# Transposing the normed rows on TensorE instead of by DMA, with row 32 of W loaded later and new instruction orders

## The chip, the core and the metric

The kernel runs on one core of a Trainium2 chip. A core has TensorE (called PE in the profile; its weight loads are PEld), VectorE (DVE), ScalarE (ACT), GpSimd (POOL) and SyncE (SP), each with its own in-order stream of instructions, the memories SBUF and PSUM (eight banks of 128 x 512 float32), and 16 DMA engines that serve the transfers that the engines issue. The metric is the time of one execution on the device in microseconds; the kernel before takes 343.75 us, the median of three runs (343.66 to 343.83).

## What is computed

The input x has 2048 rows of 512 values in bf16. Two layers are applied, each a spectral part A and a mixing MLP B, and each part adds to its own input:

```python
def A(x, w_r, w_i):                       # after a layer norm
    X = rfft2(x)                          # over rows and columns
    return irfft2(X * (w_r + 1j * w_i))   # W is 2048 x 257
def B(x, w1, w2, w3, w4):                 # after a layer norm
    h = gelu(layernorm(x) @ w1)           # 512 x 512
    hs = shifted(h) @ w2                  # four column groups, rows shifted by 1, -1, 2, -2
    x1 = x + hs
    return x1 + gelu(layernorm(x1) @ w3) @ w4   # 512 x 1792, 1792 x 512
for _ in range(2):
    x = x + A(layernorm(x), w_r, w_i)
    x = x + B(layernorm(x), w1, w2, w3, w4)
```

## The kernel before

The 2048 rows lie in SBUF as 16 groups of 128 (`K.x[:, q, :]`, called row q below; row 16p + q of x is on partition p). Everything stays in SBUF; x, W, tables and weights come in once by DMA, and only the last x goes out.

The rows' Fourier transform, the columns' transform, the product with W, and the inverse transforms are all matmuls with tables. In the first front, `scaled_T` multiplies the table T with each row's inverse standard deviation (operation Q in the orders), `front` (O) multiplies it with two rows at once on TensorE, and `take_front` (G, L, I) brings the result from PSUM to V, split between ACT and DVE. The transform proper follows: d and q (matmuls at lines 588 to 612), t and x (their evictions), p (the product with W), b (line 642), m and l (evictions into hT), D and C (line 662), Y (eviction), P (line 690) and a (adds to x, line 698).

The MLP begins with the norm of each row: s sums the squares on ACT (line 303), r works out the scale on POOL, n normalizes a row into the tile xn on ACT, DVE or POOL. The product with w1 needs the normed rows with their columns on partitions. Therefore `tr` (T) transposes two rows, one DMA for eight 128 x 128 blocks, into a tile xT that holds four rows:

```python
def turn(to, k, rows):
    ...
    nc.sync.dma_start_transpose(to[g][:, 2 * h:2 * h + 2].rearrange("p q t c -> p (q t) c"),
                                rows.rearrange("p q d -> p (q d)"))
```

v multiplies w1 with xT (line 733, 512 columns), h is the gelu into hT, u multiplies with w2 (line 749), f adds (line 757). The second norm (k, R, o) is followed by a second transpose, `tr3` (U, eight per layer, also line 718), and then by w (line 784), g (gelu into gT, line 791), W (line 804) and A (adds to x, line 810). E adds the middle of the MLP to x. In layer 1, S, Q, O, G and so on then begin the next layer's front, interleaved with the last w and W; in layer 2, y stores the rows.

No scheduler orders this. `ORDER_0` (first front), `ORDER_A` (layer 1) and `ORDER_B` (layer 2) list the operations, and each engine executes its share in the order of that list, waiting on semaphores. In an entry such as `n5A` the number is the row or unit, and a last letter A, V, P or D says which engine does it (ACT, DVE, POOL, or DVE directly from PSUM); in `w3.6` the 6 is the first PSUM bank. `X5.0` issues five filler matmuls on zeros; thirty more run at the start (`WAKE`). The letters in `FLEX` are those that carry an engine.

SP's queue issues the eight loads of x, then sixteen of W, then, after the small transfer gate2 that waits for the last doubling of W (lines 185 and 210), the tables G and Tinv and the weights w1, w2, w3, then the transposes in their order, w4 behind the eighth transpose of layer 1 (`load_w4`), and the stores. ACT's queue issues the table T and the two loads of row 32 of W (line 175) at the start. POOL's queue issues the tables FL, TL and TR at the entry f2 of ORDER_0 (`load_tables`) and the doubling copies of W after the first front (`load_rest`).

Of the kernel before, what the change touches and what calls it, by code (L numbers as in the profile page):

```python
# [28 lines left out]
def dft_tables():  # L29
# [39 lines left out]
    for j in range(NH):  # L69
        for sg in range(2):  # L70
# [26 lines left out]
           "Tinv": np.stack([T.T, -T.T], axis=1)}  # L97
# [59 lines left out]
def load_all(K, A_x, A_w_r, A_w_i, B_w1, B_w2, B_w3, B_w4):  # L157
    nc = K.nc
# [15 lines left out]
    for pl, v in enumerate(planes):  # L174
        nc.scalar.dma_start(K.W[2::4, pl, 0], v[:, 32])
    for lo in range(0, NH, 8):
        for pl, v in enumerate(planes):
            load_W(K, v, pl, lo, lo + 8)
    K.TL = K.const.tile([P, 2, NB, P], BF16, name="TL")
# [28 lines left out]
    def load_mlp():  # L208
        gate2 = K.const.tile([1, 16], BF16, name="gate2")
        nc.sync.dma_start(gate2[:], K.W[1:2, 1, NH - 1, 1:17])  # L210
        for k in ("G", "Tinv"):
            table(k, nc.sync)
        for k, w, n, c in (("w1", B_w1, 4, D), ("w2", B_w2, 4, D), ("w3", B_w3, 4, FH), ("w4", B_w4, 14, D)):
            t = K.const.tile([P, n, c], BF16, name=k)
            setattr(K, k, t)
            if k != "w4":
                load_halves(t, w, n)

    def load_w4():
        load_halves(K.w4, B_w4, 14)  # L220
# [5 lines left out]

    K.load_w4 = load_w4
# [260 lines left out]
def first_front(K):  # L488
# [66 lines left out]
    dummy = K.const.tile([P, 1, P], BF16, name="dummy")  # L555
    K.nc.sync.dma_start_transpose(dummy[:], K.zeros[:])
# [11 lines left out]
def layer(K, last):  # L568
# [144 lines left out]
    def turn(to, k, rows):  # L713

        g, h = divmod(k, 2)
        if g not in to:
            to[g] = K.grp.tile([P, 4, 4, P], BF16, name="xT", bufs=4)
        nc.sync.dma_start_transpose(to[g][:, 2 * h:2 * h + 2].rearrange("p q t c -> p (q t) c"),
                                    rows.rearrange("p q d -> p (q d)"))

    def tr(k):
        turn(xT, k, xn[:, 2 * k:2 * k + 2, :])
        turned.append(k)
        if len(turned) == 8 and not last:
            K.load_w4()
# [48 lines left out]
    def tr3(k):  # L774
        q = ROWS[2 * k]
        turn(xT3, k, xn[:, q:q + 2, :])
# [84 lines left out]
    def act_table(k):  # L861
# [42 lines left out]
FLEX = "mlGLnotxYIKEpQ"  # L904
FOLD = [(), ()]
ORDER_0 = """
s1 f0 s0 s3 s2 i3 i2 i0 s4 s5 S1 J1 s7 S0 J0 s6 i7 f2 Q2A Q3A i4 Q0A s9 i6 s8 O1.2 s11 f3 S2 J2 Q6P Q1A Q5A O0.4 i8
G1A Q4V O2.0 s10 i11 i10 S3 Q7P O3.2 G0A s13 J3 Q10V Q11A s12 s14 i12 O5.6 i14 G3A i13 G2A Q8P Q9P s15 S4 J4 O4.4 G5A
i15 Q12V Q13V S5 O6.0 L5A J5 Q14P O7.6 G4A G6A G3V Q15V L6V G7A O8.0 L7A G8A I3V L8A
"""  # L910
ORDER_A = """
d0.3 t0A d2.4 d1.2 d4.0 q0.6 t1V N0 t2A q1.2 d6.4 t4A q2.0 x1V x0V p1V t6A q4.2 d12.6 d10.4 x2A p2P p0V t12A t10A d8.0
p4D b0.6 d14.7 q10.4 m0V q6.2 t8A x10A t14A b1.0 b5.1 m5A m1A q12.4 q14.6 p6D b4.1 b2.0 p10V x14A p14P d15.2 m4A m2A
t15A q8.6 x8A b3.1 b7.0 m7A b11.2 q15.6 m11A x15A b10.3 b14.0 m3A b6.2 m6A p12D V12.4 b12.5 p8V p15V b13.7 b9.1 m10A
m12A b8.6 b15.2 m13V V15.3 m14V m9A m8V V13.5 V14.0 m15A D1.6 l12V D0.1 l15A l13A l14V C1 C0 Y0V Y1A D3.3 C3 P3.0 a3
P2.6 Y3A a2 s3 P0.5 a0 s2 P1.2 a1 s0 D2.0 C2 Y2V s1 r0 D5.6 C5 P7.2 a7 Y5A e0 s7 P6.4 D7.0 P4.5 a6 i0 M0 P5.2 D4.6 C4
P10.3 s6 C7 n2P a4 s4 a5 n3V n0V s5 Y4A D6.4 r1 P11.2 C6 P8.6 P9.7 e1 n1V a10 T1 Y7A P15.0 i1 M1 n5A s10 n4P n6P P14.1
Y6V P13.3 a8 s8 T0 a9 n7P s9 a11 P12.4 a15 s11 v1.6 r2 n10P T2 h1 T3 a13 a12 n11V c0 s15 T5 n8V v0.2 h0 s13 v3.4 n9V
v2.2 h3 u0.0 s12 h2 u1.4 a14 c1 s14 T4 u3.1 r3 f0 k0 n14V v5.2 n13A n15V T7 f1 E1V h5 f3 v4.6 u2.0 f2 E2V h4 c2 u6.6
f6 u5.5 f5 E5V k3 E6V n12P u7.0 E0V u4.1 f4 T6 v7.5 k2 k1 R0 E3V o2V o1V h7 o3A c3 v6.1 h6 o0P f7 u8.0 f8 E8P u13.5  # L920
u12.2 u11.6 u14.3 U1 f12 k4 k5 k7 f14 E14V k12 k6 u9.2 f11 u10.4 k8 E7V f13 k13 f10 R1 o7P o5P u15.3 E10V U0 w4.0 E4P
f9 E9P k11 f15 w2.4 g2 k10 o4V U2 w1.2 k14 g4 E15P k9 E13P w3.6 g3 g1 w5.0 w0.4 g0 w6.6 g5 g6 E11V W1.2 o6P U3 E12V A1
W3.6 A3 B3 B1 w8.0 W2.4 A2 W0.2 k15 R2 o10P o11A R3 o14V o9A g8 o12A w13.0 U5 w7.6 B2 g13 o8P U4 w15.4 w10.0 A0 B0 g10
w16.2 j1 g7 g16 w18.0 g18 w9.2 o15P w11.0 g9 w12.2 g12 j3 w17.6 j2 j0 S0 Q3V Q1V Q2P Q0V g11 W4.2 U7 O1.0 o13P g17 U6
A4 W7.3 B4 j4 G1A G1V A7 B7 j7 O0.0 w19.6 G0A W6.2 A6 g19 W5.3 A5 g15 B5 w23.4 g23 j5 B6 j6 S1 Q4P G0V w27.2 g27 I0V
w14.6 g14 Q5V O2.0 w20.2 w24.6 g20 W10.2 A10 B10 Q7V j10 W8.3 G2A A8 B8 W9.4 A9 B9 Q6V j9 W11.2 A11 w26.4 I1P B11 j11
g24 j8 O3.2 w22.6 S2 Q10P g26 G2V I2P Q11A Q8P g22 w21.0 g21 G3A w25.6 G3V g25 W12.0 A12 B12 j12 Q9P S12 J12 I3P O4.5
G4A Q12A G4V W15.1 A15 I4P B15 j15 W13.2 A13 S15 J15 B13 j13 W14.3 Q15P W24.2 S13 J13 Q13P O5.0 A14 A24 B14 B24 j14
G5A O15.4 G15V O6.2 S14 J14 L15A Q14A O14.4 G6A L6A G14A G5V I5V L14A
"""  # L930
ORDER_B = """
X6.7 d4.4 d15.7 t15A d12.2 t4V d1.0 d0.1 q15.4 t1V q4.6 t12A x15V q1.2 t0A x4A d2.0 p15P p1D q0.4 p0D q12.6 d10.2 t2A
x12A d8.0 q2.4 d6.6 t10A b1.3 p4V b5.2 t8A t6A q8.0 m1A m5A q6.6 p12P p2D x6A q10.3 b0.2 x10A b3.5 b2.6 m2A b4.7 m4A
d14.4 t14A p8D b9.1 m9A b13.0 p6V b12.3 p10V b7.6 m13A m7A m0A b6.4 q14.0 b15.7 b10.6 m3V b8.2 b11.5 m15A p14D b14.7
m12A m8V m14V V12.0 V14.1 V15.3 V13.2 m10A m6A l14V m11A l12A D2.5 l15V l13A D3.0 C3 Y3A C2 D1.2 C1 Y2V Y1A P7.1 a7
P6.0 a6 P4.5 P5.7 P2.2 P3.3 D0.0 s7 a4 s6 C0 a5 D5.4 s4 s5 r1 C5 a3 s3 Y0V D6.6 a2 e1 P0.0 P1.2 i1 a0 a1 Y5A P10.1 M1
n4V n5P D4.4 C4 P11.0 s2 T2 s0 n7V n6V T3 s1 r0 a10 a11 Y4A C6 e0 i0 D7.2 C7 P9.1 Y6A M0 n0P P8.4 Y7A P12.0 s11 n1V T0
a8 s10 P13.5 a9 s9 n3V n2P T1 c0 P15.2 a15 s8 P14.3 a14 s15 r2 n11V v3.1 h3 v2.3 h2 v0.6 h0 n10P T5 v1.2 a13 s13 n8P
h1 u0.4 s14 n9V T4 u3.5 a12 c1 u1.0 s12 r3 f3 u2.7 f1 k1 n14V n15P T7 f0 v5.2 c3 f2 v4.0 n13A h5 u4.3 n12V T6 f4 E3V
k0 h4 E1V u6.7 c2 u7.6 f7 k3 E0V u5.1 k2 R0 E7V E2V o1P o2P f5 E5V k4 v6.5 h6 o0A v7.0 h7 u13.6 o3V U1 u12.4 u15.5 f6  # L940
E6P f13 E13P u14.3 f14 k7 k5 E14V k6 R1 o7A E4V u11.0 f15 f12 k14 k12 u9.2 E15P f9 k13 o6V u8.1 u10.3 f10 E10V f11
E11V k15 U0 w6.4 w4.2 g4 k9 f8 E8V R3 o15A E12V o13V k10 w5.0 w1.2 g5 o12P k11 g1 w2.6 w0.1 g2 o14V g0 k8 R2 o11V o8P
w3.6 U3 g3 o5A U6 U7 w26.0 w21.2 g21 w22.6 g26 w23.2 E9V o9P g6 W0.0 A0 o4V U2 W3.1 W2.0 g23 g22 w25.2 W1.4 g25 w11.2
# [34 lines left out]
```

## Time and profile before

| | |
|---|---|
| median of three runs | 343.75 us (343.66 to 343.83) |
| profiled execution | 343.63 us, its span 341.8 us |
| TensorE busy | 334.3 us, 2184 matmuls |
| ACT, DVE, POOL busy | 192.0, 163.5, 117.5 us |
| granted TensorE clock | 1.00 throughout |
| DMA transposes | 32, 3.1 us each from issue to landing |

The profile shows one execution. Busy time of TensorE rests on modelled ends of matmuls, so the rate is read from how many matmuls pass in a stretch. "Idle before" in the groups is how long the engine stood still before these instructions, with what released it. The chain of waits is followed back from the last instruction, and a row of it gives start, length, engine, line and count. The groups by form keep different shapes of one line apart. The windows give each engine's busy time in a stretch of the span.

### The profile page before, as it was taken

How to read it: one execution, taken by the hardware profiler on the slowest of the kernel's cores; microseconds unless marked ns; L12 is line 12 of the kernel's file. 1: busy time of each engine (PE TensorE's matmuls, PEld its weight loads, DVE VectorE, ACT ScalarE, POOL GpSimd, SP SyncE). 2: the span in 40 equal slices, each digit the busy share in tenths (PEclk: the TensorE clock that was granted, in tenths of full speed). 3: DMA queues.
4: the chain of work that ended last, by engine and by line, in shares of the span. 5: the costliest groups of instructions: out<-in, count | busy, mean ns of one | idle time of the engine just before them, and what ended most of it. 6: DMA issues, size and time to landing. Idle time of an engine off the chain costs nothing.

```text
span 341.8 us, 5734 instructions
## 1 busy us (share of the span) xinstructions
PE 334.3 (98%) x2184; PEld 186.8 (55%) x2184; DVE 163.5 (48%) x373; ACT 192.0 (56%) x356; POOL 117.5 (34%) x218
## 2 busy tenths in 40 slices
PE   6999999999999999999999999999999999999996
PEld 4878984444444444444467898444444444444443
DVE  4979895659034023535378979456901110200112
ACT  6989899665821542421628979986695132142310
POOL 3795067669633000402432505877722000000000
PEclk9999999999999999999999999999999999999999
DMA  7985936390231100000000003543130500000011
GB/s 261 313 284 197 339 78 117 71 270 19 46 61 31 32 0 0 2 0 0 2 0 2 2 3 64 104 83 61 33 61 0 125 31 0 15 17 32 15 63 46
DMA packets 45340, 24.60 MB, mean 72 GB/s; under 512 B 35153, under 2 KB 42321, under 8 KB 45313
## 3 DMA queue, kind: packets, MB, share of 16 engines
q1 hardware_dynamic: 43824, 19.74, 23.0%
q0 software_dynamic: 1248, 4.40, 3.9%
q8 instruction: 17, 0.28, 0.3%
q10 hardware_dynamic: 240, 0.10, 0.1%
q14 instruction: 11, 0.08, 0.1%
HBM read 11.61 MB, written 2.10 MB: 40 GB/s over the span
## 4 chain that ended last, share of the span: by engine, by line
PE 85%; ACT 8%; DVE 3%; DMA 2%; issue 1%; SPq 0%; ACTq 0%
PE ps L804 28%; PE ps L784 28%; PE ps L749 8%; PE ps L733 6%; PE ps L642 4%; ACT xn L303 3%; PE ps L612 2%; PE ps L594 2%; DVE x_state L698 2%; PE ps L662 2%; DMA x_state<-in_A_x_dram 1%; ACT hT L740 1%; DMA xT<-xn 1%; PE ps L439 1%; PE ps L429 1%
## 5 line engine op out<-in xcount | busy, mean ns | idle before, releaser
L791 ACT ACTIVATE gT<-ps 128x1024 bf16<-128x1024 f32 x56 | 55.7, 1023 | 97.6 <-PE ps L784 95.5
L804 PE MATMUL ps<-w,gT 128*128 128x512 bf16 (+2 forms) x476 | 99.4, 366 | 0.0
L784 PE MATMUL ps<-xT,w 128*128 128x512 bf16 x448 | 99.3, 379 | 0.0
L810 DVE TENSOR_TENSOR x_state<-ps,x_state 128x512 bf16<-128x512 f32 (+2 forms) x34 | 22.1, 659 | 123.4 <-PE ps L804 123.1
L804 PEld LDWEIGHTS <-gT 128*128 128x128 bf16 x476 | 45.4, 98 | 51.4
L784 PEld LDWEIGHTS <-w 128*128 128x128 bf16 x448 | 43.7, 98 | 52.1
L757 DVE SCALAR_TENSOR_TENSOR xn<-xn,ln_c,ps 128x512 bf16<-128x512 bf16 x32 | 23.3, 742 | 16.0 <-PE ps L749 6.3
L733 PE MATMUL ps<-xT,w 128*128 128x512 bf16 x128 | 28.6, 379 | 0.4 <-DMA xT<-xn 0.4
L749 PE MATMUL ps<-w,hT 128*128 128x512 bf16 x128 | 28.8, 379 | 0.1
L326 POOL TENSOR_SCALAR ln_ve<-ln_mv 128x4 f32<-128x4 f32 x11 | 3.0, 271 | 57.7 <-DVE ln_mv L319 57.0
L303 ACT ACTIVATE junk<-xn 128x512 bf16<-128x512 bf16 x32 | 19.8, 623 | 5.0 <-DVE xn L757 5.0
L291 DVE BATCH_NORM_STATS2 ln_st<-x_state 128x6 f32<-128x512 bf16 (+2 forms) x30 | 19.5, 665 | 3.5 <-DMA x_state<-in_A_x_dram 3.0
L698 DVE SCALAR_TENSOR_TENSOR x_state<-ps,x_state 128x512 bf16<-128x512 f32 x32 | 20.6, 684 | 0.9 <-PE ps L690 0.9
L733 PEld LDWEIGHTS <-w 128*128 128x128 bf16 x128 | 12.4, 98 | 15.6 <-DMA xT<-xn 1.0
L749 PEld LDWEIGHTS <-hT 128*128 128x128 bf16 x128 | 12.5, 98 | 15.4 <-ACT hT L740 1.0
L303 ACT ACTIVATE xn<-x_state 128x512 bf16<-128x512 bf16 x32 | 19.9, 626 | 0.8 <-DVE x_state L698 0.8
L740 ACT ACTIVATE hT<-ps 128x512 bf16<-128x512 f32 x32 | 17.6, 600 | 4.6 <-PE ps L733 4.5
L690 PE MATMUL ps<-Y,Tinv 128*128 128x256 bf16 x128 | 15.8, 272 | 0.4 <-DVE Y L152 0.4
L631 POOL TENSOR_TENSOR PB<-X,W 128x2048 bf16<-128x2048 bf16 (+1 forms) x4 | 12.1, 3033 | 11.2 <-DVE X L152 7.3
L154 ACT ACTIVATE TV<-ps 128x1024 bf16<-128x1024 f32 (+1 forms) x17 | 14.6, 895 | 2.4 <-PE ps L594 2.3
L642 PE MATMUL ps<-TR,PB 128*128 128x128 bf16 x256 | 15.9, 219 | 0.0
L662 PE MATMUL ps<-G,hT 128*128 128x256 bf16 x128 | 15.6, 273 | 0.0
(96 smaller groups left out, 414.0 us busy)
## 6 DMA issues: line engine op xcount, KB each, us to landing
w<-in_B_w_dram SPq DMA_DIRECT2D x4, 896.0 KB, 7.0
W<-W POOLq DMA_DIRECT2D x4, 514.0 KB, 5.1
x_state<-in_A_x_dram SPq DMA_DIRECT2D x8, 256.0 KB, 4.9
out_dram<-x_state SPq DMA_DIRECT2D x15, 128.0 KB, 1.8
w<-in_B_w_dram SPq DMA_DIRECT2D x4, 256.0 KB, 4.4
W<-in_A_w_r_dram SPq DMA_DIRECT2D x7, 128.5 KB, 5.4
W<-in_A_w_i_dram SPq DMA_DIRECT2D x7, 128.5 KB, 5.6
TL<-tab_TL POOLq DMA_DIRECT2D x3, 256.0 KB, 5.5
```

Of the source, the lines that this page charges most:

```text
L303: K.nc.scalar.activation(out, src, ACT.Square, bias=0.0, scale=D ** -0.5, accum_out=self.s[:, i, 1:2])
L642: nc.tensor.matmul(o[:, k0 * P:(k0 + 1) * P], lhsT=pab[u][:, k, 2 * (b - u) + h, f * P:(f + 1) * P], rhs=K.TR[:, k:k + 2, 2 * b + h], star ...
L662: nc.tensor.matmul(o[:, i, e * 256:(e + 1) * 256], lhsT=M[:, F, e, 2 * m + i, :], rhs=K.G[:, F, e, :], start=(F == 0 and e == 0), stop=(F ...
L698: nc.vector.scalar_tensor_tensor(K.x[:, q, :], ps.pop(("P", q)), 1.0, K.x[:, q, :], op0=ALU.mult, op1=ALU.add, accum_out=ln[g].s[:, i, 0:1])
L733: nc.tensor.matmul(o[:, i], lhsT=K.w1[:, t, j * P:(j + 1) * P], rhs=xT[g][:, :, t, :], start=(t == 0), stop=(t == 3))
L740: nc.scalar.activation(hv[:, 2 * h + i, 4 * g:4 * g + 4, PAD:PAD + P], o[:, i].rearrange("p (q c) -> p q c", q=4), ACT.Gelu_apprx_tanh, bi ...
L749: nc.tensor.matmul(o, lhsT=K.hT[:, j, st:st + P], rhs=K.w2[:, j, :], start=(j == 0), stop=(j == 3))
L757: nc.vector.scalar_tensor_tensor(xn[:, q, :], xn[:, q, :], ln[q // 4].c[:, q % 4:q % 4 + 1], ps.pop(("u", n)), op0=ALU.mult, op1=ALU.add, ...
L784: nc.tensor.matmul(o[:, i], lhsT=K.w3[:, c, t * P:(t + 1) * P], rhs=xT3[g][:, :, c, :], start=(c == 0), stop=(c == 3))
L791: nc.scalar.activation(gT[g][:, 2 * j:2 * j + 2, :], ps.pop(("w", k)), ACT.Gelu_apprx_tanh, bias=0.0, scale=1.0)
L804: nc.tensor.matmul(o, lhsT=gT[g][:, t, i * P:(i + 1) * P], rhs=K.w4[:, t, d], start=(t == 0), stop=(t == 13))
L810: nc.vector.tensor_tensor(x, ps.pop(("W", n)), x, op=ALU.add)
```

## The change

The turn is done by matmuls: eight for a pair of rows, each with a 128 x 128 block of rows as the stationary operand and the unit matrix as the moving one, into two PSUM banks. One copy of 128 x 1024 then brings it from PSUM to xT, on ACT or DVE; it is a new entry of the order, Z for the first and F for the second norm. The unit matrix is one more table, loaded on SP behind Tinv. The transposing DMA `dummy`, issued once ahead of the others, is gone, and w4 is loaded straight behind w3. Row 32 of W is loaded on SP behind the first four loads of W. All three orders are new: beside the Z and F entries they change the sequence throughout, and deal some operations to other engines (in layer 1, for instance, nine norms n go to POOL instead of six and five to DVE instead of eight). Layer 1 gets five fillers at its beginning, and layer 2 loses six.

```diff
-           "Tinv": np.stack([T.T, -T.T], axis=1)}
+           "Tinv": np.stack([T.T, -T.T], axis=1), "unit": np.eye(P)}
...
-    for pl, v in enumerate(planes):
-        nc.scalar.dma_start(K.W[2::4, pl, 0], v[:, 32])
     for lo in range(0, NH, 8):
         for pl, v in enumerate(planes):
             load_W(K, v, pl, lo, lo + 8)
+        if lo == 0:
+            for pl, v in enumerate(planes):
+                nc.sync.dma_start(K.W[2::4, pl, 0], v[:, 32])
...
-        for k in ("G", "Tinv"):
+        for k in ("G", "Tinv", "unit"):
             table(k, nc.sync)
         for k, w, n, c in (("w1", B_w1, 4, D), ("w2", B_w2, 4, D), ("w3", B_w3, 4, FH), ("w4", B_w4, 14, D)):
             t = K.const.tile([P, n, c], BF16, name=k)
             setattr(K, k, t)
-            if k != "w4":
-                load_halves(t, w, n)
-
-    def load_w4():
-        load_halves(K.w4, B_w4, 14)
+            load_halves(t, w, n)
...
-    dummy = K.const.tile([P, 1, P], BF16, name="dummy")
-    K.nc.sync.dma_start_transpose(dummy[:], K.zeros[:])
...
-    def turn(to, k, rows):
-
-        g, h = divmod(k, 2)
+    def turn(key, rows):
+
+        ps[key] = o = banks(K, 2)
+        for i in range(2):
+            for t in range(4):
+                nc.tensor.matmul(o[:, i, t * P:(t + 1) * P], lhsT=rows[:, i, t * P:(t + 1) * P], rhs=K.unit[:],
+                                 start=True, stop=True)
+
+    def take_turned(to, key, eng):
+        g, h = divmod(key[1], 2)
         if g not in to:
             to[g] = K.grp.tile([P, 4, 4, P], BF16, name="xT", bufs=4)
-        nc.sync.dma_start_transpose(to[g][:, 2 * h:2 * h + 2].rearrange("p q t c -> p (q t) c"),
-                                    rows.rearrange("p q d -> p (q d)"))
+        copy(K, to[g][:, 2 * h:2 * h + 2].rearrange("p q t c -> p q (t c)"), ps.pop(key), eng)
 
     def tr(k):
-        turn(xT, k, xn[:, 2 * k:2 * k + 2, :])
-        turned.append(k)
-        if len(turned) == 8 and not last:
-            K.load_w4()
+        turn(("T", k), xn[:, 2 * k:2 * k + 2, :])
...
     def tr3(k):
         q = ROWS[2 * k]
-        turn(xT3, k, xn[:, q:q + 2, :])
+        turn(("U", k), xn[:, q:q + 2, :])
...
-             "T": tr, "v": w1, "h": gelu1, "u": w2, "f": add_x1, "k": square3, "E": resid,
+             "T": tr, "Z": lambda k, eng: take_turned(xT, ("T", k), eng), "F": lambda k, eng: take_turned(xT3, ("U", k), eng), "v": w1, "h": gelu1, "u": w2, "f": add_x1, "k": square3, "E": resid,
...
-FLEX = "mlGLnotxYIKEpQ"
+FLEX = "mlGLnotxYIKEpQZF"
 ORDER_0 = """
-s1 f0 s0 s3 s2 i3 i2 i0 s4 s5 S1 J1 s7 S0 J0 s6 i7 f2 Q2A Q3A i4 Q0A s9 i6 s8 O1.2 s11 f3 S2 J2 Q6P Q1A Q5A O0.4 i8
...
+s1 f0 s0 i0 s2 i2 s3 i3 s8 s5 S0 J0 S1 J1 s9 s10 i8 s11 Q2A Q3A O1.6 i10 Q1A s12 i11 Q0P s15 f3 S3 J3 Q10A i12 s13 s4
+Q11A i13 s7 i4 Q8A O0.1 G0A s6 i6 S4 G1A J4 Q12V i7 Q9P O5.3 f2 L5A s14 S2 J2 Q4V Q7V i15 Q13A O4.0 Q6P O6.6 i14 Q5P
...
 ORDER_A = """
-d0.3 t0A d2.4 d1.2 d4.0 q0.6 t1V N0 t2A q1.2 d6.4 t4A q2.0 x1V x0V p1V t6A q4.2 d12.6 d10.4 x2A p2P p0V t12A t10A d8.0
...
-P10.3 s6 C7 n2P a4 s4 a5 n3V n0V s5 Y4A D6.4 r1 P11.2 C6 P8.6 P9.7 e1 n1V a10 T1 Y7A P15.0 i1 M1 n5A s10 n4P n6P P14.1
-Y6V P13.3 a8 s8 T0 a9 n7P s9 a11 P12.4 a15 s11 v1.6 r2 n10P T2 h1 T3 a13 a12 n11V c0 s15 T5 n8V v0.2 h0 s13 v3.4 n9V
...
+X5.0 d1.0 d0.1 t0A d2.2 t2A d10.6 t10A N0 t1V q0.4 q1.0 p0D q2.2 d6.6 d14.4 x2A d15.5 q10.2 p1D t6A q6.0 t14A q14.6
...
+a6 P4.7 a4 Y5V Y4A D6.0 n0V C6 s6 n1P P14.5 P8.4 P15.6 P9.7 s4 T0.2 Y6A P12.1 P13.0 a15 r1 e1 i1 n3A a9 a8 n2P T1.6
+a14 M1 n6P Z0A Z1A P10.2 a10 P11.3 a11 s8 s9 n7P s10 s11 n5V T3.4 Z3V a12 v1.6 h1 n4P r2 n8P n9P c1 T2.2 Z2V v0.4 v3.2
...
 ORDER_B = """
-X6.7 d4.4 d15.7 t15A d12.2 t4V d1.0 d0.1 q15.4 t1V q4.6 t12A x15V q1.2 t0A x4A d2.0 p15P p1D q0.4 p0D q12.6 d10.2 t2A
...
+d0.2 d1.0 t1V d15.4 d12.6 q1.0 t0A d4.2 p1D t15A t12A t4A q0.4 d2.6 q15.0 t2A p0D q4.2 q12.4 d6.6 x15V p4D d8.0 x12A
...
```

## The prediction

> **What bounds the kernel now.** I read the busy row of the page first, then the chain of waits, then the groups by form, then windows of time, because the busy row alone can't be trusted for TensorE: ends of matmuls are modelled in it.
>
> ```profile
> PE 334.3 (98%) x2184; PEld 186.8 (55%) x2184; DVE 163.5 (48%) x373; ACT 192.0 (56%) x356; POOL 117.5 (34%) x218
> PE 85%; ACT 8%; DVE 3%; DMA 2%; issue 1%; SPq 0%; ACTq 0%
> ```
>
> TensorE is named by both. How full it really is I work out from its true rate, which the chain of waits shows in runs of equal matmuls:
>
> ```profile
> 97.37 1.73 PE ps L784 x8
> 178.35 0.45 PE ps L439 x8
> 199.53 2.62 PE ps L662 x24
> ```
>
> The first row gives 216 ns for a 512-column matmul, the third 109 ns for 256 columns, the second 56 ns for 128 columns, where every matmul has its own weight load. (The "mean ns" column says 379, 273 and 219 for the same three: that is latency, not rate.) The groups by form count 1124 matmuls of 512 columns (L784, L804, L749, L733), 28 of 384 (4.9/28, at most 0.17 each), 392 of 256, 476 of 128, 128 half-height ones at L612 (16 in 0.98 us of the chain, 0.061 each) and 36 fillers of 256. So the streams need 242.8 + 4.6 + 42.7 + 26.7 + 7.8 + 3.9 = 328.5 us. The first matmul starts at 1.0 us and the last ends at 339.1: of 338.1 us only about 10 are not streaming. The start holds 4 of them: 30 fillers worth 3.3 us stand in the 7.2 us before the first real matmul at 8.23. **Some 6 us are left in the other 330.**
>
> ```profile
> 8.23 2.14 PE L429 MATMUL ps<-Tq,x_state 128*128 128x256 bf16 x24 [1.90 <-ACT Tq L412]
> ```
>
> Where those 6 lie, windows of time tell (columns: window, length, then busy us and count of PE, PEld, DVE, ACT, POOL, then the granted clock, the DMA share, GB/s):
>
> ```profile
> 8.20:19.00 10.80, 10.04 (x121) 9.03 (x120) 10.28 (x35) 10.76 (x25) 8.86 (x15) 1.00 1.01 321
> 19.00:36.00 17.00, 16.88 (x244) 13.92 (x245) 14.74 (x19) 15.89 (x26) 10.94 (x10) 1.00 0.70 229
> 36.00:62.00 26.00, 25.74 (x193) 17.86 (x191) 18.12 (x49) 23.15 (x55) 13.58 (x34) 1.00 0.59 160
> 62.00:180.00 118.00, 118.00 (x607) 56.22 (x606) 52.96 (x125) 51.46 (x85) 40.05 (x69) 1.00 0.17 38
> 200.00:216.00 16.00, 15.26 (x131) 12.53 (x130) 13.05 (x37) 14.14 (x34) 6.68 (x18) 1.00 0.31 56
> ```
>
> From 62 us to 180 us (and again after 216) TensorE never pauses and the others idle half the time. Only in the first front (to 19 us), the transforms and the first half of the MLP are ACT and DVE nearly full beside it. The clock is 1.00 throughout.
>
> **What the DMA transposes cost now.** Their rows:
>
> ```profile
> xT<-xn SPq DMA_TRANSPOSE x32, 3.1
> L733 PE MATMUL ps<-xT,w 128*128 128x512 bf16 x128 | 28.6, 379 | 0.4 <-DMA xT<-xn 0.4
> 211.02 3.50 DMA xT<-xn
> ```
>
> 32 transposes, 3.1 us each from issue to landing, and TensorE idles for them 0.4 us in all; one stands on the chain, at the start of layer 2's MLP. Their work is on the DMA engines and SP, which are free. So the removal gives back 0.4 us, with what surrounds that one wait at most 0.7 (16.00 less 15.26 in the last window shown above).
>
> **Added: turns on TensorE.** Each of 8 turns of xn and 8 of the second norm, in 2 layers, makes 8 matmuls, a stationary 128x128 block each, against the unit matrix: 32 x 8 = 256 matmuls of 128 columns. The nearest row is L439: 8 matmuls, the stationary operand a 128x128 block of bf16 rows, 128 columns moving, 0.45 us. 32 x 0.45 = **14.4 us**, on the engine that has no room: half of it falls in w3 and W work where no pause exists, half beside norms where pauses come to about 1 us a layer. Here a rule has to be weighed. The Trainium skill ("TensorE: Matmul & The Clock Gate", Part 4: PE-mode transpose) measures 390 ns for such a transpose in isolation and about 275 ns within a kernel, and says the clock gate doesn't count that mode as work. By 275 ns, 256 turns are an estimated 70 us, and the kernel ends near 414. I take the row: it is the rate of back-to-back ordinary matmuls, and the diff uses ordinary ones; 275 resembles the row's latency of 219 ns, which pipelining hides. A second page looks only at the pair of engines: "VectorE: DVE Perf Modes" (Rules for kernel authors, with its three transpose paths) prefers TensorE, 390 against 1309 ns for DMA. By that 256 x 919 ns = 235 us would be an estimated saving; the wait row allows 0.4. A price off the path can't be saved.
>
> **Added: copies.** 32 evictions of 128x1024 f32. Rows of the same shape:
>
> ```profile
> L154 ACT ACTIVATE Y<-ps 128x1024 bf16<-128x1024 f32 x11 | 11.1, 1015 | 2.6 <-PE ps L662 1.4 <-issue 1.1
> L152 DVE CAST Y<-ps 128x1024 bf16<-128x1024 f32 x5 | 6.1, 1223 | 3.1 <-PE ps L662 3.0
> ```
>
> The new orders put 16 on ACT (16.2 us), 16 on DVE (19.6). The second norm's 16 stand beside w3, where both engines idle half the time: nothing. The first norm's in layer 1 are 4 on ACT (4.06 us) and 4 on DVE, in a stretch where the chain runs from 40.85 to 59.43 through ACT and TensorE has no pause either. TensorE grows by 8 x 0.45 = 3.6 there, ACT by 4.1: the difference, **0.4**; between 0 (three normings more go to POOL) and 2 (a copy waits for its turn behind a gelu of two 0.6 us pieces, with v queued behind it on TensorE). In layer 2 only 2 of 8 are on ACT, so TensorE stays the longer one. A turn plus its copy, 0.45 + 1.0 to 1.2, is shorter than 3.1 us plus the 1.25 us of an SP issue, so the wait at 211 should shrink: **-0.5**, between -0.7 and +1 (an unready norm now holds TensorE itself, where before it held SP's queue only: u and v stand behind the turn).
>
> **New order of the first front.** ACT is full in that window (10.76 of 10.80), so its order sets when V is whole. Before, ACT makes the first two row scalings (Q2, Q3) before row 9's sums:
>
> ```profile
> 7.67 1.30 ACT L412 ACTIVATE Tq<-T,ln_r 128x256 bf16<-128x256 bf16 x3
> 8.88 0.61 ACT L366 ACTIVATE junk<-x_state 128x512 bf16<-128x512 bf16 x1
> 15.72 3.41 ACT L154 ACTIVATE V<-ps 128x512 bf16<-128x512 f32 x7
> ```
>
> Now s9 stands ahead of Q2, and s8 on DVE ahead of J0. Rows 8 and 9 are in the fifth load of x: issued near 2.6 us, landed after 4.9 to 5.3, so 7.5 to 7.9. ACT then sums for 1.3 us and begins Q2 near 9.2 instead of 7.67. The sums aren't lost (they'd have come at 8.88), so the loss is ACT's idleness: 0.3 us waiting for rows 8 and 9, and about 1 us before S3, whose group now waits on DVE for s8, J0, J1, s10, s11 and two aggregations. One scaling more (0.46) and one take fewer (0.6 to 0.9) cancel. +1.3, less what earlier x gives: row 32's two issues leave ACT's queue, 33 KB, 0.1 us at 321 GB/s, up to 0.5 if such small packets hold the queues longer than their bytes. I take **+0.9**, between -0.5 and +2.0. The five fillers ahead of layer 1 lie in that wait; six fewer at layer 2: **-0.1** by count (36 to 35 at 109 ns), up to -0.7.
>
> **Moved issues.** Row 32's two loads take 0.62 us each on SP, ahead of 12 W loads: these issue 1.25 us later. What they feed waits on POOL's doubling copies, the first at 17.1 us; row 32 should land by about 13.5, with 3.5 us cover; if it were gone, the transforms would start that much later. POOL's tables (FL, TL, TR) are issued at f2, which now stands behind f3, Q0, Q9: near 12.7 instead of 7.95. At the old 5.7 us FL lands near 18.4, at 2 to 3 us less without queueing; the transform wants it near 20. TL's second half follows 2.4 us of POOL work and could be late for q10, which the new order takes fourth: **+0.3**, between -0.5 and +1.5, for the whole transform stretch with its re-dealt takes. W4's load goes from behind the eighth transpose to behind w3, 0.9 MB twice, long before W at 91 us; the unit matrix (32 KB, one SP issue of 0.43) delays w1 by as much, and v starts at 51 us, over ten later than w1's landing: both nothing.
>
> **Sum.** 14.4 + 0.4 - 0.5 + 0.9 - 0.1 + 0.3 = 15.4 us. The profiled execution took 343.63 with a span of 341.8; it becomes 359.0 with a span of 357.2. The median of the runs is 343.75, 0.1 above it: **359.1 us**.
>
> **Rivals.** (1) The new orders also take back pauses: half of the 6 us that remain outside the start. For it: ACT in the chain at 40 to 59, the pauses in 200 to 216. Against: after 62 us there is nothing to take. 355.4 to 357.6, chance 0.16. (2) The copies make ACT or DVE the bound in both norm stretches, each copy on ACT (6 of 1.0) with half the waits: +2 to +4 over the forecast, 361 to 363.5; for it 23.15 of 26.00 on ACT; against it DVE's 18.12. Chance 0.13. (3) The first front loses its full 2 us and late tables another: 361 to 362.5, chance 0.10. (4) The page's 275 ns rules: 414; 0.02. (5) The other side: the turns slip into TensorE's pauses, as the modelled ends hide idle time in the norm stretches. It decides when pauses worth 14.4 us lie there; my count by rates finds 6 outside the start. Were it true, 343.5; chance 0.01. The forecast itself, 357.6 to 360.6, has 0.58.
>
> **Range.** Adding the low bounds gives about 355.4, the high ones about 364; 8 in 10 is 356.4 to 362.6. A measurement tells changes beyond about 0.2% (0.7 us): slower 0.98, same 0.01, faster 0.01.
>
> **What would show it.** Right: a new TensorE line with 256 matmuls at 0.45 us per eight, the 512-column runs unchanged at 216 ns, still no pause after the first norm, no DMA transposes, ACT about 16 us busier, DVE less than 20, and the first front's matmuls beginning after 9 us. Wrong: turns at 0.1 us or more each, or TensorE pauses of several us before v or w3 with a copy named as releaser (rival 2), or a transform stretch that starts at 19 us or earlier (then rival 1).

## The result, and the profile after

The changed kernel takes **361.41 us** (median of four runs, 361.04 to 362.46) against 343.71 for the kernel before (343.62 to 343.83, run beside it on the same chip). The ratio is 1.052, its 95% interval 1.0498 to 1.0542: 17.7 us slower. The profiled execution took 361.43 us with a span of 359.7.

The busy row and the row of the chain's shares, from the page of the kernel after:

```profile
PE 350.1 (97%) x2439; PEld 202.7 (56%) x2439; DVE 181.6 (50%) x388; ACT 209.2 (58%) x374; POOL 105.6 (29%) x215
PE 91%; ACT 4%; DMA 2%; DVE 2%; issue 1%; ACTq 0%
```

TensorE has 255 matmuls more (256 turns, one filler fewer) and its share of the chain has risen from 85% to 91%. The bound is the same engine, with more to do. ACT is 17.2 us busier, DVE 18.1. What was added shows in the groups by form (busy time, mean ns of one, idle time before and its releaser):

```profile
L152 DVE CAST xT<-ps 128x1024 bf16<-128x1024 f32 x16 | 19.4, 1218 | 10.3 <-PE ps L711 6.1
L154 ACT ACTIVATE xT<-ps 128x1024 bf16<-128x1024 f32 x16 | 16.1, 1021 | 11.0 <-PE ps L711 11.0
L711 PE MATMUL ps<-unit,xn 128*128 128x128 bf16 x256 | 18.5, 219 | 0.0
```

The copies wait for the turns, not the turns for anything: 0.0 us idle before L711. The 18.5 us and 219 ns of the last row are latency again. The rate is read in the chain of waits (start, length, line, count), where equal matmuls follow each other:

```profile
53.59 0.45 PE ps L711 x8
...
99.63 3.02 PE ps L800 x14
102.66 0.89 PE ps L711 x16
```

A turn takes 0.45 us, 56 ns a matmul, and the 512-column stream of L800 keeps its 216 ns. From start to start the 256 turning matmuls sum to 14.40 us. Windows of the kernel after (columns as in the prediction):

```profile
9.70:21.90 12.20, 12.09 (x126) 10.61 (x125) 10.06 (x32) 9.98 (x21) 9.36 (x19) 0.86 0.86 252
21.90:41.15 19.25, 18.22 (x256) 15.09 (x257) 17.38 (x21) 17.24 (x29) 4.03 (x7) 1.00 0.82 275
41.15:68.00 26.85, 26.85 (x224) 19.83 (x224) 19.95 (x49) 24.57 (x54) 13.83 (x34) 1.00 0.32 110
68.00:190.00 122.00, 122.00 (x680) 60.19 (x678) 57.06 (x137) 56.68 (x91) 35.46 (x64) 1.00 0.00 1
210.70:230.00 19.30, 19.30 (x177) 15.77 (x176) 17.57 (x41) 16.29 (x37) 7.43 (x21) 1.00 0.01 2
```

From 41 us on TensorE is busy in 26.85 of 26.85, 122.00 of 122.00 and, in layer 2's norm stretch, 19.30 of 19.30 us. There the kernel before still had pauses. The extra loss lies in the first two rows: the first front runs at a clock of 0.86, and the first transform has about 1 us of TensorE pauses where the kernel before had 0.12 in its 17 us.

Marks in the two traces give a ledger. "Rows" is the first row matmul, D1 and D2 the first inverse column transform (line 662 before, 655 after) of each layer, d1 and d2 the first forward one:

| mark or stage, us | before | after | difference | forecast |
|---|---|---|---|---|
| rows begin | 8.23 | 9.73 | +1.50 | |
| rows to d1 | 10.73 | 12.16 | +1.43 | |
| transform 1, d1 to D1 | 17.89 | 19.26 | +1.37 | |
| together, start to D1 | 36.85 | 41.15 | **+4.30** | +1.2 |
| layer 1, D1 to d2 | 145.23 | 151.72 | +6.49 | 7.2 turns + 0.4 - 0.1 = +7.5 |
| transform 2, d2 to D2 | 17.28 | 17.87 | +0.59 | 0 |
| layer 2, D2 to the last matmul's end | 139.74 | 145.80 | +6.06 | 7.2 turns - 0.5 = +6.7 |
| behind the last matmul | 2.70 | 3.12 | +0.42 | 0 |
| span | 341.80 | 359.66 | +17.86 | +15.4 |

So the turns cost about what they were forecast to, the layers took back more than forecast, and the first 41 us lost 3.1 us more than forecast.

What happens in the first front is seen in the timeline of the kernel after (start, length, engine, line, and in brackets the idle time before it with its releaser):

```profile
7.95 0.63 ACT L361 ACTIVATE junk<-x_state 128x512 bf16<-128x512 bf16 x1
...
9.19 1.29 ACT L407 ACTIVATE Tq<-T,ln_r 128x256 bf16<-128x256 bf16 x3
...
13.18 0.82 POOL L190 DMA_DIRECT2D FL<-tab_FL  x1
...
17.25 1.62 POOL L405 TENSOR_SCALAR Tq<-T,ln_r 128x128 bf16<-128x128 bf16 x2 [1.43 <-DVE ln_r L389]
18.82 0.66 POOL L186 DMA_DIRECT2D W<-W  x1
...
22.13 0.41 DVE L152 CAST V<-ps 128x256 bf16<-128x256 f32 x1
...
25.06 2.35 DVE L621 TENSOR_TENSOR PB<-ps,W 128x1024 bf16<-128x1024 f32 x2 [1.23 <-PE ps L605]
```

ACT sums a row of the fifth load of x at 7.95 and scales its first row only at 9.19. POOL issues its first table at 13.18 and its first doubling of W at 18.82. DVE writes the last piece of V at 22.13, so that V is whole at 22.54. The same steps in the kernel before:

```profile
7.95 0.82 POOL L189 DMA_DIRECT2D FL<-tab_FL  x1
...
17.09 0.67 POOL L185 DMA_DIRECT2D W<-W  x1
...
18.03 1.12 DVE L471 TENSOR_TENSOR V<-pairs 128x256 bf16<-128x256 f32 x2
...
23.24 1.29 DVE L631 TENSOR_TENSOR PB<-X,W 128x1024 bf16<-128x1024 bf16 x2
```

There V was whole at 19.15. So the 4.30 us at D1 are 3.39 for V and 0.91 for what follows it (18.61 us from V to D1 instead of 17.70). The chain of waits of the kernel after passes through V, by way of the scalings, the row matmuls and the takes into V (start, length, engine, line):

```profile
9.29 0.41 ACT Tq L407
...
9.73 4.30 PE ps L424 x32
...
22.20 0.35 DVE V L152
...
22.60 0.23 PE ps L583
```

Neither a table nor the doubling of W is on it there. The doubling stands close behind, though. Issued 5.2 us later, FL landed at 18.0 instead of 13.7. The first doubling of W, issued 1.7 us later, landed 3.7 us later, at 24.86 instead of 21.18, and DVE's first product with W began 0.2 us behind it (the kernel before left 2.1 us between the two). POOL had stood idle for 1.43 us between its tables and the doubling: it waited for DVE's `ln_r`, which two row scalings ahead of the doubling need.

### The profile page after: what moved, and what is told of

Read it like the earlier page. It is cut to its first block, busy times and chain, and to the rows that moved or that the text cites. A ratio compares the mean times of both kernels' runs of the same rounds, so it can differ in the third digit from the quotient of the medians.

```text
span 359.7 us, 6165 instructions
## 1 busy us (share of the span) xinstructions
PE 350.1 (97%) x2439; PEld 202.7 (56%) x2439; DVE 181.6 (50%) x388; ACT 209.2 (58%) x374; POOL 105.6 (29%) x215
## 4 chain that ended last, share of the span: by engine, by line
PE 91%; ACT 4%; DMA 2%; DVE 2%; issue 1%; ACTq 0%
PE ps L800 27%; PE ps L780 27%; PE ps L729 8%; PE ps L745 8%; PE ps L711 4%; PE ps L683 4%; PE ps L655 4%; PE ps L635 4%; PE ps L605 2%; ACT TV L154 1%; PE ps L587 1%; PE ps L424 1%; DMA x_state<-in_A_x_dram 1%; ACT V L154 1%; DMA T<-tab_T 1%; PE ps L434 1%
## 5 line engine op out<-in xcount | busy, mean ns | idle before, releaser
L780 PE MATMUL ps<-xT,w 128*128 128x512 bf16 x448 | 100.0, 379 | 0.0
L800 PE MATMUL ps<-w,gT 128*128 128x512 bf16 (+2 forms) x476 | 99.9, 366 | 0.0
L787 ACT ACTIVATE gT<-ps 128x1024 bf16<-128x1024 f32 x56 | 56.0, 1024 | 74.3 <-PE ps L780 74.0
L800 PEld LDWEIGHTS <-gT 128*128 128x128 bf16 x476 | 45.3, 98 | 49.9
L745 PE MATMUL ps<-w,hT 128*128 128x512 bf16 x128 | 30.4, 379 | 0.0
L729 PE MATMUL ps<-xT,w 128*128 128x512 bf16 x128 | 29.4, 379 | 0.0
L152 DVE CAST xT<-ps 128x1024 bf16<-128x1024 f32 x16 | 19.4, 1218 | 10.3 <-PE ps L711 6.1
L154 ACT ACTIVATE xT<-ps 128x1024 bf16<-128x1024 f32 x16 | 16.1, 1021 | 11.0 <-PE ps L711 11.0
L621 DVE TENSOR_TENSOR PB<-ps,W 128x1024 bf16<-128x1024 f32 x17 | 19.9, 1217 | 2.1 <-PE ps L605 1.9
L711 PEld LDWEIGHTS <-xn 128*128 128x128 bf16 x256 | 16.5, 98 | 5.1 <-ACT xn L397 0.2
L745 PEld LDWEIGHTS <-hT 128*128 128x128 bf16 x128 | 12.2, 98 | 12.7
L304 POOL TENSOR_SCALAR ln_mv<-ln_s 128x4 f32<-128x4 f32 x16 | 4.2, 260 | 50.8 <-DVE x_state L691 40.9
L711 PE MATMUL ps<-unit,xn 128*128 128x128 bf16 x256 | 18.5, 219 | 0.0
```

Of the source, the lines that this page charges most:

```text
L154: K.nc.scalar.activation(dst, src, ACT.Copy, bias=0.0, scale=1.0)
L621: nc.vector.tensor_tensor(t[:, :, 2 * i:2 * i + 2], o[:, :, i * 256:(i + 1) * 256].unsqueeze(1).to_broadcast([P, 2, 2, 256]), K.W[:, :, 2 ...
L711: nc.tensor.matmul(o[:, i, t * P:(t + 1) * P], lhsT=rows[:, i, t * P:(t + 1) * P], rhs=K.unit[:], start=True, stop=True)
L729: nc.tensor.matmul(o[:, i], lhsT=K.w1[:, t, j * P:(j + 1) * P], rhs=xT[g][:, :, t, :], start=(t == 0), stop=(t == 3))
L745: nc.tensor.matmul(o, lhsT=K.hT[:, j, st:st + P], rhs=K.w2[:, j, :], start=(j == 0), stop=(j == 3))
L780: nc.tensor.matmul(o[:, i], lhsT=K.w3[:, c, t * P:(t + 1) * P], rhs=xT3[g][:, :, c, :], start=(c == 0), stop=(c == 3))
```

## The experiments

The theory, A where an expectation names it: the turns' 14.4 us lie wholly on TensorE's path, their copies are covered, and the excess over the forecast is made in the first front, by its late start, its slow clock or its late tables. The rivals, B and others in the expectations, put the loss elsewhere: the copies hold TensorE, the new sequences cost or save time by themselves, or the turn is dearer than its rate. No kernel here leaves anything of the computation out. Two repeat a piece of work, and are named as such. Times are medians; ratios are to the kernel before, run on the same chip.

### Turns and copies in the old orders

The entries Z and F, with two banks a turn, are put into the three orders of the kernel before, and row 32 stays on ACT's queue:

```diff
-P10.3 s6 C7 n2P a4 s4 a5 n3V n0V s5 Y4A D6.4 r1 P11.2 C6 P8.6 P9.7 e1 n1V a10 T1 Y7A ...
+P10.3 s6 C7 n2P a4 s4 a5 n3V n0V s5 Y4A T1.4 Z1A D6.4 r1 P11.2 C6 P8.6 P9.7 e1 n1V a10 Y7A T0.0 Z0A ...
```

> The turns alone: TensorE turns, one copy to a pair and w4 behind w3, but the three orders of before (each turn and its copy set in where its rows are ready) and row 32 of W on ACT's queue as before. Theory A (the turns cost their TensorE time of 14.4 us, and what is beyond it comes from the new order of the first front): 358.1 to 360 us, first row matmul at 8.2 us and transform at 19.0 as before. Theory B (the copies load ACT and DVE, and the first front's lateness is absorbed later): 361 us or more.

It took 399.27 us (397.36 to 399.97), ratio 1.1597 (1.1558 to 1.1637): 55.5 us more than before, 41 of them beyond the turns. TensorE's waits in this kernel (line waited at, releaser: total us, times, longest):

```profile
PE ps L779 <- ACT xT L154: 7.8, 4, 2.6
PE ps L779 <- DVE xT L152: 6.0, 2, 4.6
...
PE ps L744 <- DVE xT L152: 2.9, 1, 2.9
```

L779 is w3, L744 the product with w2. They wait for a copy; w3 reads it, and the product with w2 doesn't, so there it is probably the bank that still holds a turn. Theory A missed, and B's "361 us or more" is met, but by far too much for the reason that it gives: this doesn't isolate the turn, it shows that a turn needs room around it. Up to D1 the kernel kept the old marks (rows at 8.02, d1 at 18.75, D1 at 37.08). So the early loss of the change doesn't come with the turns.

### The first order alone put back

The changed kernel with ORDER_0 of the kernel before:

```diff
 ORDER_0 = """
-s1 f0 s0 i0 s2 i2 s3 i3 s8 s5 S0 J0 S1 J1 s9 s10 i8 s11 Q2A Q3A O1.6 ...
+s1 f0 s0 s3 s2 i3 i2 i0 s4 s5 S1 J1 s7 S0 J0 s6 i7 f2 Q2A Q3A i4 Q0A s9 ...
```

> The changed kernel with ORDER_0 of before, all else as changed. Theory A: the first row matmul comes back from 9.7 to about 8.2 us, the transform's start from 22.6 to about 19, and the time falls by 3 to 3.6 us to 357.8 to 358.4. Theory B: the transform starts earlier, but the time stays within 0.7 us of 361.4 because ACT and DVE bound the norm stage. Theory C (row 32 moved to SP makes x late): the start stays late by 0.4 us or more, 359 to 361.

360.51 us (360.15 to 362.1), ratio 1.0488 (1.0458 to 1.0519): hardly better, and outside the ranges of A and B. It lies in C's, and the rows begin at 8.63, 0.4 us late as C had it; but with row 32 still on SP they began at 8.00 in the kernel with TL early, below. The front is repaired, with d1 at 19.79 instead of 21.89, and the gain is lost at once: D1 is at 41.63. The timeline of TensorE in this kernel shows where:

```profile
26.91 1.16 PE L605 MATMUL ps<-TV,TL 64*128 64x256 bf16 x18 [1.86 <-DMA TL<-tab_TL]
...
29.04 0.63 PE L587 MATMUL ps<-FL,V 128*128 128x256 bf16 x2
29.47 0.31 PE L581 MATMUL ps<-FL,V 128*128 128x128 bf16 x1
```

q10, fourth in the new layer 1, waits 1.86 us for the second half of TL, and behind that pause two 256-column matmuls need 0.43 us from start to start, twice their usual 0.22. The table's lateness is a second limit behind the first.

### The late start and the slow clock

The run at full clock until the row matmuls begin, with 36 fillers more; then, separately, row 32 put back on ACT's queue:

```diff
-WAKE = 30
+WAKE = 66
```

> The changed kernel with 66 fillers at the start in place of 30, so that TensorE is never idle before its first row matmul. If TensorE's idle 4 us before 9.7 us is what makes the next 32 matmuls take 213 ns for 256 columns in place of 109: these return to 109 ns, the granted clock of the second 10 us returns from 0.83 to 1.00, and the time falls by 0.8 to 1.7 us to 359.7 to 360.6. If the late row scalings alone make the loss: 361.2 to 361.6, with the same slow matmuls or with waits in their place.

```diff
+    for pl, v in enumerate(planes):
+        nc.scalar.dma_start(K.W[2::4, pl, 0], v[:, 32])
...
-        if lo == 0:
-            for pl, v in enumerate(planes):
-                nc.sync.dma_start(K.W[2::4, pl, 0], v[:, 32])
```

> The changed kernel with the two loads of row 32 of W back at the start on ACT's queue. Theory A: no difference, 361.1 to 361.7. Theory C: x lands some 0.4 us earlier (first rows at 3.9 in place of 4.3 us) and the time falls to 360.5 to 361.0. Against both, if the loads in ACT's queue delay the fifth load of x: slower by 0.2 to 0.5.

With the fillers 361.24 us (360.51 to 361.52), ratio 1.0494: the clock was back at 1.00, the fillers overran the start (rows at 10.84), d1 came at 21.51 and D1 at 41.25; DVE's first product with W waited 1.32 us for the doubling. With row 32 early 360.79 us (359.89 to 362.78), ratio 1.0495, rows at 9.63, D1 at 40.84: the median is in C's range, but the spread of the runs covers A's too. Neither the clock nor row 32 holds the time by itself.

### The turns by DMA in the new orders

The turn of the kernel before inside the new sequences; Z and F issue nothing:

```diff
     def turn(key, rows):
-        ps[key] = o = banks(K, 2)
-        for i in range(2):
...
+        nc.sync.dma_start_transpose(to[g][:, 2 * h:2 * h + 2].rearrange("p q t c -> p (q t) c"),
+                                    rows.rearrange("p q d -> p (q d)"))
     def take_turned(to, key, eng):
+        return
```

> The changed kernel with its new orders, but each turn made by the transposing DMA of before and the entries Z and F empty. Theory A (the turns cost their TensorE time, 14.4 us, and nothing else in the MLP does): 361.4 less 14.4 is 347.0, with up to 3 us of waits since the new orders leave a turn less lead than a DMA of 3.1 us needs: 347 to 350. Theory B (part of the turns lies in TensorE's pauses, and the new orders cost the rest): 351 or more.

359.82 us (359.53 to 361.25), ratio 1.0483, in B's range: 14.4 us of matmuls gone, 1.6 us gained. TensorE's waits in this kernel:

```profile
PE ps L729 <- DMA xT<-xn: 4.9, 2, 2.6
...
PE ps L780 <- DMA xT<-xn: 2.7, 3, 1.8
```

The new sequences put the product close behind its turn, which suits 0.45 us and a copy, and not a DMA of 3.1. The waits listed sum to 7.6 us. Soon after two of them (2.59 us before 57.95, and 2.27 before 225.6 in layer 2) some eight matmuls of 512 columns took 427 ns from start to start instead of 216. The first 41 us are as in the kernel after: V is whole at 22.56, D1 at 41.17. So that loss doesn't come with the turns either. Like the first experiment, its mirror image, it says that turn and sequence belong together; the two can't be priced by swapping one.

### Old first order, and TL's second half early

The limit found with the first order put back is taken away: the load moves from behind the doublings to the end of `load_tables`.

```diff
 ORDER_0: as in the kernel before
     def load_tables(...):
+        q.dma_start(K.TL[:, 1, 8:16], dram["TL2"])
...
     def load_rest(...):
-        q.dma_start(K.TL[:, 1, 8:16], dram["TL2"])
```

> The changed kernel with ORDER_0 of before, and the second half of the second TL table loaded with the first tables instead of behind the doubling of W. If the wait of 2.1 us for that table, and the slow matmuls after it, are what ate the gain of the earlier first front: the wait is gone, the inverse transform starts near 38.6 us in place of 41.6, and the time falls to 357.3 to 358.2. If ACT and DVE bound the transform of the new order whatever lands: 360 to 361.

**358.86 us** (358.45 to 359.89), ratio 1.0451 (1.0433 to 1.0469), the fastest version of the changed kernel, though 0.7 above the range expected. In its timeline the tables and the doubling are issued as early as in the kernel before, and the product with W is earlier than there:

```profile
7.72 0.82 POOL L190 DMA_DIRECT2D FL<-tab_FL  x1
...
17.05 0.67 POOL L186 DMA_DIRECT2D W<-W  x1
...
21.87 2.35 DVE L621 TENSOR_TENSOR PB<-ps,W 128x1024 bf16<-128x1024 f32 x2 [1.24 <-PE ps L605]
```

V is whole at 19.11, D1 is at 38.02 instead of 41.15, and that is kept to the end: the last matmul ends at 353.68 instead of 356.54. Against the kernel before it ends 14.58 us later (353.68 less 339.10), which is the turns and 0.2 us; that it is so little comes of an offset, since 1.17 us at D1 and 0.59 in transform 2 remain and the two layers take back nearly as much. So the early loss beyond about 1.2 us can be taken back without touching the turns.

### The turns twice, and in another mode

Each turn's matmuls are issued a second time into the same banks (work repeated); then the same turns as TensorE transposes, into one bank of bf16:

```diff
-        for i in range(2):
+        for i in (0, 1, 0, 1):
```

> The changed kernel with each turn's eight matmuls issued twice, the second time over the first. Theory A (every turn stands on the path that sets the end): 14.4 us more, 375.3 to 376.3. Theory B (half of them lie in pauses or beside ACT and DVE): 7 to 10 us more, 368 to 371.

```diff
-        ps[key] = o = banks(K, 2)
+        ps[key] = o = banks(K, 2)[:, 0].bitcast(BF16).rearrange("p (i d) -> p i d", i=2)
...
-                nc.tensor.matmul(o[:, i, t * P:(t + 1) * P], lhsT=rows[:, i, t * P:(t + 1) * P], rhs=K.unit[:],
-                                 start=True, stop=True)
+                nc.tensor.transpose(o[:, i, t * P:(t + 1) * P], rows[:, i, t * P:(t + 1) * P], K.unit[:])
```

> The changed kernel with TensorE's transpose operation in place of ordinary matmuls against the unit matrix; its output stays bf16, so a pair of rows takes one PSUM bank. If a transpose streams like any 128-column matmul: 56 ns each and 360.6 to 361.6, a little less if the copy from bf16 is quicker. By the page's 275 ns each: 256 more of 219 ns, 56 us more, near 417.

Twice: 375.72 us (375.1 to 376.52), ratio 1.0939, in A's range, 14.3 over the kernel after for 256 more matmuls:

```profile
L711 PE MATMUL ps<-unit,xn 128*128 128x128 bf16 x512 | 32.8, 219 | 0.0
```

Another 56 ns each (14.3/256), all of it on the path. That is the disputed price, measured by itself.

As transposes: 361.89 us (361.6 to 362.78), ratio 1.0532 (1.0514 to 1.055), not told apart from the kernel after, just above the first range expected and far from 417. The groups by form of this kernel:

```profile
L154 ACT ACTIVATE xT<-ps 128x1024 bf16<-128x1024 bf16 x16 | 16.1, 1020 | 11.0 <-PE ps L711 11.0
L711 PE MATMUL ps<-unit,xn 128*128 128x128 bf16 x256 | 18.5, 219 | 0.0
L152 DVE COPY xT<-ps 128x1024 bf16<-128x1024 bf16 x16 | 10.9, 685 | 11.5 <-PE ps L711 11.4
```

From start to start the 256 transposes sum to 14.36 us, 56 ns each, at a granted clock of 0.99. DVE's copies shrank from 1218 to 685 ns, and the time stayed: from D1 to the end of the last matmul it is 315.3 us, 315.4 in the kernel after. The single copies are covered.

### The copies twice

Each copy is made a second time (work repeated):

```diff
-        copy(K, to[g][:, 2 * h:2 * h + 2]..., ps.pop(key), eng)
+        for o in (ps[key], ps.pop(key)):
+            copy(K, to[g][:, 2 * h:2 * h + 2]..., o, eng)
```

> The changed kernel with each copy from PSUM made twice. Theory A (the copies lie beside TensorE's work): 16 more of 1.02 us on ACT and 16 of 1.22 on DVE cost at most 1.5 us, in the norm stretches: 361.4 to 363. Theory B (the copies bound the norm stretches): 4 more on ACT in layer 1 and 6 on DVE in layer 2 stand on the path there: 366 to 373.

375.96 us (374.4 to 377.6), ratio 1.0919: 14.5 over the kernel after, above what A and B allowed. TensorE's waits in this kernel:

```profile
PE ps L730 <- DVE xT L152: 5.2, 5, 1.4
...
PE ps L781 <- DVE xT L152: 2.0, 3, 0.9
PE ps L683 <- DVE xT L152: 1.7, 2, 1.1
...
PE ps L683 <- ACT xT L154: 1.0, 1, 1.0
```

The products with w1 (L730), w3 (L781) and the inverse row transform (L683) now wait for copies. From D1 to the first w3 layer 1 grew by 5.8 us, layer 2 by 6.9, and the rest behind D1 by about 1.9. So the cover of a copy is real but thin: for single copies of 1.0 to 1.2 us no wait of TensorE showed, and doubled ones of 2.0 to 2.4 cost 0.45 us each on average (14.5/32).

### Three more edits of the first front

All three have TL's second half early, and keep the new ORDER_0; the second adds 25 fillers, the third moves four sums behind the first scalings:

```diff
+        q.dma_start(K.TL[:, 1, 8:16], dram["TL2"])
```

> The changed kernel, new first order too, with the second half of the second TL table loaded with the first tables. In the changed kernel it lands at 27.0 us and is used at 27.5, so it should not matter there: 361.0 to 361.7, the transform starting near 21.9 and the inverse one near 41.1. If it binds even so: 360.5 or less. It is the base of the next two.

```diff
-WAKE = 30
+WAKE = 55
```

> As the run before it, with 55 fillers instead of 30, ending near 9.5 us. If the slow matmuls after TensorE's idle 4 us are part of the first front's loss: rows from 9.7 us at 109 ns, the transform starts at 20.3 to 21.0 in place of 21.9 and the time falls by 0.9 to 1.6 us. If ACT's takes bound the front whatever the clock: the transform starts at 21.5 to 22 and the time stays within 0.4 us.

```diff
-s1 f0 s0 i0 s2 i2 s3 i3 s8 s5 S0 J0 S1 J1 s9 s10 i8 s11 Q2A Q3A O1.6 i10 Q1A ...
+s1 f0 s0 i0 s2 i2 s3 i3 s5 S0 J0 S1 J1 Q2A Q3A O1.6 s8 s9 s10 i8 s11 i10 Q1A ...
```

> The run before the last (table early), with the sums of rows 8 and 9 moved behind the first two scalings in the new first order, and nothing else. If they are what makes the front late: first row matmul at 8.0 to 8.6 us at full rate, the transform starts at 19.5 to 20.4, and the time falls by 1.5 to 2.4 us to 359.0 to 359.9. If the rest of the new first order is: the first matmul comes early, but the transform starts at 21.3 or later and the time stays above 360.8.

| us | time | ratio's interval | rows | V whole | d1 | D1 |
|---|---|---|---|---|---|---|
| after | 361.41 | 1.0498 to 1.0542 | 9.73 | 22.54 | 21.89 | 41.15 |
| TL early | 361.26 | 1.0492 to 1.0528 | 9.37 | 22.29 | 21.77 | 40.91 |
| and 25 fillers | 361.39 | 1.0495 to 1.0526 | 10.17 | 22.15 | 21.41 | 41.40 |
| and sums later | 360.94 | 1.0482 to 1.0513 | 8.46 | 21.08 | 21.13 | 40.81 |
| old first order, TL early | 358.86 | 1.0433 to 1.0469 | 8.00 | 19.11 | 19.36 | 38.02 |

The times of all three came out where their expectations put the case that the edit does little. The third begins 1.27 us ahead of the kernel after, nearly as early as the kernel before, and has 0.34 us of that left at D1. Two lines of its timeline say why:

```profile
8.46 2.84 PE L424 MATMUL ps<-Tq,x_state 128*128 128x256 bf16 x32 [1.41 <-ACT Tq L407]
...
25.35 2.36 DVE L621 TENSOR_TENSOR PB<-ps,W 128x1024 bf16<-128x1024 f32 x2 [1.59 <-DMA W<-W]
```

The rows start early, and then DVE stands 1.59 us for the doubling of W. In the other two it waits for the same transfer, 1.64 and 1.81 us, and starts its first product at 25.28 and 25.95. In all of these, and in the kernel after, D1 follows that start by 15.4 to 16.1 us (41.15 less 25.06, for one); with the tables early (21.87, D1 at 38.02) by 16.2. So two limits stand one behind the other, V and the doubling. In the kernel after they lie 0.2 us apart, so a repair of one alone can hardly gain anything.

This holds for the new layer 1, which makes its products with W sooner after V. In the old one (the kernel before, and the turns in the old orders) the first product began at 23.24 and 23.10, and D1 followed by 13.6 and 14.0 us. And V itself is late for more than the sums: with these moved, the clock whole and the rows at 8.46 it still came 1.9 us later than before.

## Why the prediction was right or wrong

The forecast was 359.1 us, the range 356.4 to 362.6; 361.41 lies within, 2.3 above the forecast and outside the likeliest case's own 357.6 to 360.6. It is where rival 3 stood (first front and late tables, 361 to 362.5, chance 0.10), and partly for rival 3's reasons. That the sum missed by so little is partly luck: the first 41 us lost 3.1 more than forecast and two stretches without a term another 1.0, while the layers gave back 1.65 more. The low and high bounds of the terms add up to 355.7 and 364.5, not 355.4 and 364; the range stated doesn't hang on that.

**The bound: right.** TensorE was the engine with no room from 41 us to the end, and the 14.3 us of the doubled turns show that any matmul added there is paid in full.

**The turns: right in size.** 32 x 0.45 us were forecast, 14.40 were measured, and 56 ns for each matmul held in two kernels and in another mode. The rule weighed against the row, about 275 ns for a transpose within a kernel in the Trainium skill ("TensorE: Matmul & The Clock Gate", Part 4: PE-mode transpose), would by the prediction's estimate have put the time at about 414; even with the transpose mode that it speaks of, the runs gave 361.89. Latency was 219 ns throughout, so the row's rate was the right one to count with. The skill's other page, with its preference for TensorE ("VectorE: DVE Perf Modes", Rules for kernel authors), gained nothing, as the wait row had said.

**The copies: right by result, the reason too generous.** No copy shows as a wait of TensorE in layer 1's window (26.85 of 26.85), so +0.4 was, if anything, too much. But "both engines idle half the time: nothing" reads cover from busy shares. What counts is the time between a turn and the next matmul that needs its rows or its banks, and the doubled copies found it shorter than two copies.

**Pauses given back: right in kind, too small.** The -0.5 for layer 2 was measured as -1.1 (6.06 less the 7.2 of the turns). The prediction took the 0.7 us that the windows show idle around 200 to 216 as the limit. The distances between starts of TensorE's matmuls in the trace before give 1.23 us of pauses from 206 to 214 (0.60, 0.17 and 0.46 beyond the rate of what ran), since the modelled ends cover part of each; the trace after has none of the three. In layer 1, 0.7 us came back too, again from pauses: 0.32 us before the first product with w1 and 0.27 on a gelu in the norm stretch of the trace before, and 0.1 later. The six fillers gave back hardly anything, as the -0.1 had it: their 0.66 ahead of d2 is gone, but the row matmuls there take 0.60 more from start to start, with two waits on DVE.

**The first front and the moved tables: the terms that were mis-sized.** +0.9 and +0.3 were forecast, +4.30 was measured at D1. The +0.9 stands against V, whole 3.39 us later, and the +0.3 for "the whole transform stretch with its re-dealt takes" against the 0.91 from V to D1. The prediction's account of the start came true: s9 ahead of Q2, the fifth load of x landing at 7.87, the scaling at 9.19, the matmuls "after 9 us" at 9.73. Moving the sums, which also left the clock whole, brought V forward by 1.2 us (22.29 to 21.08), near the 1.3 that was worked out. Three things were not in it. The rest of the new first order was put at nothing ("One scaling more (0.46) and one take fewer (0.6 to 0.9) cancel"), and costs V up to 1.9 us. The clock wasn't thought of: behind TensorE's longer pause, 3.4 us of row matmuls ran at half rate (what that alone costs V is not shown, since the fillers that restored the clock made the rows later). And the cover of row 32, "3.5 us", was reckoned against the old issue of the doubling, without asking when the doubling itself would now land. It landed just ahead of its first reader, and in six of the kernels run here DVE waits 1.0 to 1.8 us for it.

The moved tables themselves were foreseen well: f2 near 12.7 (13.18), FL near 18.4 (18.0); neither is on the chain of the kernel after. TL's second half, "late for q10", does bind as soon as V is early.

Open ends: of the 3.1 us that the old first order with TL early takes back, it isn't shown which part belongs to which entry of the order; f2 alone was not moved. f2's place is not what made the issue of the doubling late in the kernel after, since POOL stood idle in between. Why the doubling then took 6.0 us to land instead of 4.1 no run shows; with the turns in the old orders, where the tables are early, it took as long (16.87 to 23.02).

**Left without a term.** Transform 2 is 0.59 us longer, and 0.42 more lies behind the last matmul. The forecast had nothing there. Both belong to the new sequences and not to the turns: transform 2 takes 17.9 us in every kernel with the new orders for the layers, the one with DMA turns among them, and 17.3 with the turns in the old orders; behind the last matmul it is 3.0 to 3.3 us against 2.7. Which of the re-dealt operations make the difference is not shown.

## What to carry to other kernels

An engine with no pauses pays for every instruction added to it at its true rate, which is the distance between starts in the chain of waits and not the mean duration; what the removed work was worth is its wait row, however long the transfers took. When the order of a front is changed, follow every transfer of its queues up to its landing and its first reader; here the table that was watched cost nothing, and the doubling of W two steps further had lost its cover. And where a front is late, shortening its visible delay may only bring up the next transfer: look for the mark that the end goes with (here the first product with W), and for everything that reaches it within a fraction of a microsecond, before mending the start.

## What was not expected of the hardware

TensorE lost half its rate behind fairly short pauses. After 3.84 us of idleness ahead of the kernel after's first row matmul the rate was whole for 1.1 us, and then a 256-column matmul took 213 ns from start to start instead of 109 for 3.4 us (granted clock 0.83 from 10 to 20 us). The same was seen behind 1.86 us on the wait for TL and behind 2.59 us on a DMA turn (427 instead of 216 ns for 512 columns). Pauses of 1.41 us before the rows (sums later) and 1.90 us (before) left the rate whole, and so did 2.48 us in the kernel with turns in the old orders, 2.69 before the rows with the old first order alone, and 3.67 with the copies twice, so there is no sharp bound in these runs.

A DVE copy of 128x1024 out of PSUM took 685 ns where PSUM held bf16 and 1218 where it held float32; on ACT the same pair took 1020 and 1021 ns.
